# Another order of loads and steps, other kinds of pairs and wider copies in a retention-and-mixer kernel

## The chip, the core and the metric

One core of one Trainium2 chip runs the whole program. The metric is the device time of one execution in microseconds (us). The kernel before was timed in three runs; a fourth execution was profiled, and its own time is given beside its span (first to last instruction).

## What is computed

```python
# q, k, v: (4 batches, 8 heads, 768 tokens, 64); x: the attention output as (4, 768, 512)
gamma = 1.0 - 2.0 ** (-5.0 - np.arange(H))
for t in range(S):
    state = gamma * state + outer(k[:, :, t], v[:, :, t])      # 64 x 64 for each head
    y[:, :, t] = scale * q[:, :, t] @ state
...
wq = x @ w_q; wk = x @ w_k                                     # 512 -> 64
W_tok = scale * einsum('bsd,btd->bst', wq, wk)
mixed = einsum('bst,btd->bsd', W_tok, x)
out = np.maximum(mixed, 0.0) @ w_out                           # 512 -> 512
```

The first stage is a linear attention with a decay for each head. The second mixes all tokens of a batch without a softmax, so that it is computed through the 64 x 512 matrix wk^T x (called z) rather than through a 768 x 768 matrix.

## The kernel before

The 768 tokens of a batch are cut in three **pairs** of 256 tokens, so there are 12 pairs, 0 to 11, and three in a row make a batch. A pair has two chunks of 128 tokens, c = 0 and 1. q, k and v of a pair are 512 KB each and are loaded into one of 27 slots of a staging tile (`stage`). Products are taken in bf16 and gathered in the eight PSUM banks; bank 7 holds the running state.

All work is one list, `ORDER` (L16 to L60), that is walked once from front to back. Each token of it is a step: `name.pair.part:engine@banks=slot`. Every engine gets its steps in the order of the list and never overtakes, a step starts when what it reads is there and when what it overwrites has been read, and the semaphores for that are put in by the framework. The load queue (SP) issues its loads and the final stores in the order of the list as well. A load waits in the list for its slot to be read out and for room in the queue; where it stands among the steps of the engines does not matter. The engine letters are A (ACT), V (DVE) and P (POOL).

The steps of a pair, in the order in which its data flows:

- `Lk Lq Lv` load; `ck cv cq` cast to bf16 (`cv` also multiplies v with the inverse decay), part 0 and 1.
- `trk trq` transpose k and q on PE into one bank (eight 128x128 transposes), or, with an `a` behind the banks, into halves of two banks (sixteen 64-row ones). `ek eq` copy the results out (kT, qT).
- `sc` scores of half the heads, into two banks; `eat` multiplies them with the mask on DVE and leaves them in bf16.
- `st` adds k^T v of a chunk to the state in bank 7; `es` copies the state out.
- `ia` and `in` add the part of y within a pair and the part from the state, into two banks; `ex` scales y by the decay on DVE (x).
- `xt exT` transpose x and copy it out; `wqk ew` make wq and wk (m); `zm ez` make z of a batch; `mx` mixes; `r` applies the relu to a chunk; `pj` is the last product of a chunk (four matmuls of 512 columns); `eo` copies it to a staging slot; `S` stores.
- `fill.n@b` runs n matmuls on zeros; they keep PE busy and compute nothing. `W`, `WO` cast the weights that `LW`, `LO` load.

Each pair has a **kind** (L62), which says how its 256 tokens lie in the 128 partitions after loading. In the kinds R and 2 a partition holds two neighbouring tokens of each head, so that a DMA reads 512 B in one piece. For R the cast also moves half the rows, so that `ck` and `cv` take two instructions of 64 partitions for each part. For 2 a part is one instruction of 128 partitions, but `st` takes 16 matmuls in place of 8, `sc` and `ia` 16 in place of 8, and `in` 12 in place of 8. In M the k is loaded as in R, and v is loaded in four DMAs of 256 B pieces, which leaves `cv` one instruction a part. In N both k and v are read in 256 B pieces, and `ck` has one instruction a part as well.

Tiles come from pools of a fixed number of buffers (L69): `relu=4` buffers of one chunk each, `x=6`, `ks=6` and so on. A new tile waits until the oldest of its pool has been read for the last time.

Of the kernel before, what the change touches and what calls it, by code (L numbers as in the profile page):

```python
# [22 lines left out]
Lq.10=5 cv.3.1:P cq.5.0:P ia.0.1@56 fill.1@1 trk.2@1 fill.1@3 in.0.1@56 Lk.10=12 cq.2.1:A cq.2.0:A
sc.1.0@23 ek.2:V cv.4.0:P sc.1.1@01 trq.2@4 eq.2:A es.0.1:A ia.0.0@56 eat.1.0:V ex.0:V eat.1.1:V
cv.4.1:P fill.4@2 sc.2.1@34 cq.3.0:A cv.5.0:P sc.2.0@56 fill.2@2 st.1.0 es.1.0:A ck.3.0:A ck.3.1:A
Lv.10=6 Lq.11=8 ia.1.1@01 in.1.1@01 st.1.1 eat.2.1:V ck.6.0:P ia.1.0@01 in.1.0@01 trq.3@4 eat.2.0:V
xt.0@5 cv.5.1:P ex.1:V cq.7.1:P cq.7.0:P cv.6.1:P es.1.1:V exT.0:V eq.3:V trk.3@6 fill.2@2 in.2.0@01
cv.6.0:P Lv.11=9 st.2.0 ck.4.1:A ek.3:A xt.1@5 es.2.0:A exT.1:V ck.4.0:A ia.2.1@01 ia.2.0@01
in.2.1@01 ck.7.1:P ex.2:V st.3.0 fill.1@2 sc.3.0@56 trk.4@34a cq.4.1:A cv.7.1:P cv.7.0:P W:A trq.4@0
xt.2@1 ek.4:V sc.3.1@23 ck.8.1:P cq.8.0:P eat.3.0:V eq.4:V wqk.1@4 ew.1:V cq.5.1:A exT.2:A es.3.0:A  # L30
wqk.0@5 ck.8.0:P sc.4.0@01 trq.5@6 wqk.2@4 ck.5.1:A ew.0:A eat.4.0:V ew.2:V zm.0.0@5 sc.4.1@01
st.3.1 eat.3.1:V ck.5.0:A WO.0:A es.3.1:A trk.5@4 cq.9.1:P cv.8.0:P in.3.1@23 zm.0.1@5 ia.3.1@23
ia.3.0@23 eat.4.1:V ez.0:V cv.9.0:P cv.8.1:P st.4.0 ex.3:V ek.5:A es.4.0:A in.4.0@01 mx.0@45
in.4.1@01 ia.4.1@01 ia.4.0@01 eq.5:V WO.1:A st.4.1 xt.3@23a r.0.1:A pj.0.1@6 ex.4:V r.0.0:A es.4.1:A
ck.6.1:A eo.0.1:A=11 xt.4@01a cv.9.1:P mx.1@45 exT.3:V r.1.0:A cq.6.0:A sc.5.0@23 pj.0.0@6 st.5.0
exT.4:V r.1.1:V eat.5.0:V trk.6@4 ek.6:V sc.5.1@01 cq.6.1:A eo.0.0:A=11 trq.6@56a wqk.4@2 es.5.0:A
ia.5.0@34 eq.6:A in.5.0@34 in.5.1@34 eat.5.1:V trq.7@56a mx.2@01 ew.4:V eq.7:V r.2.1:A r.2.0:A
ck.7.0:A ia.5.1@34 wqk.3@2 ex.5:V pj.1.0@5 sc.6.1@01 st.6.0 eo.1.0:A=14 sc.6.0@34 xt.5@6 trk.7@5
ek.7:A eat.6.1:V pj.1.1@0 exT.5:V wqk.5@6 es.6.0:V st.6.1 eo.1.1:A=14 ew.5:A es.6.1:A ew.3:A
# [861 lines left out]
```

## Time and profile before

| | |
|---|---|
| three timed runs | 100.23, 100.91, 100.99 us; median 100.91 |
| the profiled execution, its own time | 100.14 us |
| its span | 98.4 us |
| granted TensorE clock, mean | 0.996 |
| busy: PE, DVE, ACT, POOL | 88.6, 74.4, 70.3, 51.8 us |
| HBM read, written | 20.19 MB, 6.29 MB |

A busy time is the union of an engine's instructions. PE's matmuls overlap in their pipeline and their ends are modelled, so the mean duration of one is longer than the step from one to the next; the step is read from rows of several in a row. PE's busy time contains the fills. DMA is the mean busy share of the 16 DMA engines of the core.

### The profile page before, as it was taken

Reading aid. Unit: us, or ns where it says so; the run is one execution under the profiler, and the core shown is the slowest. Engines: PE = TensorE matmul, PEld = TensorE weight load, DVE = VectorE, ACT = ScalarE, POOL = GpSimd, SP = SyncE. Lnnn points to the kernel's source line nnn. Section 1 sums busy time; section 2 is a strip of 40 time slices with the busy share of each in tenths; the row PEclk is TensorE's granted clock in tenths of the full one; section 3 lists DMA queues with packets and bytes.
Section 4 is the critical chain, followed back from the end, with each engine's and each line's share of the span. In section 5 each row is a group of like instructions: output and inputs, shape, how many; then the busy total and the mean of one; then the engine's idle time right before and its main releaser. Section 6 shows DMA issues by size and latency. Waiting matters only on the chain.

```text
span 98.4 us, 3827 instructions
## 1 busy us (share of the span) xinstructions
PE 88.6 (90%) x1626; PEld 59.9 (61%) x1642; DVE 74.4 (76%) x127; ACT 70.3 (71%) x124; POOL 51.8 (53%) x68
## 2 busy tenths in 40 slices
PE   5994899999869999999999988999999989999940
PEld 1333477487757776586887554786787766744410
...
DMA  1999999999998999999899799799905910690893
GB/s 26 282 385 368 367 363 361 343 327 282 293 330 256 303 317 348 354 336 293 255 337 309 177 323 323 159 244 273 361 21 205 402 46 0 245 391 14 323 397 132
DMA packets 37953, 26.73 MB, mean 272 GB/s; under 512 B 8240, under 2 KB 31792, under 8 KB 37936
## 3 DMA queue, kind: packets, MB, share of 16 engines
...
q10 hardware_dynamic: 528, 0.26, 0.9%
...
HBM read 20.19 MB, written 6.29 MB: 269 GB/s over the span
## 4 chain that ended last, share of the span: by engine, by line
PE 55%; SPq 20%; ACT 7%; DMA 6%; DVE 4%; issue 2%; POOL 1%; DVEq 0%; POOLq 0%
PE banks L826 19%; SPq L193 11%; DMA stage<-in_q_dram 6%; SPq L172 6%; PE banks L748 5%; PE banks L759 5%; PE banks L558 3%; PE banks L685 3%; SPq L200 3%; ACT relu L819 3%; PE banks L592 2%; PE banks L515 2%; PE banks L804 2%; DVE relu L821 2%; PE banks L631 2%
## 5 line engine op out<-in xcount | busy, mean ns | idle before, releaser
L401 POOL TENSOR_TENSOR vs<-stage,fv 64x512 bf16<-64x512 f32 x22 | 23.6, 1075 | 6.4 <-DMA stage<-in_v_dram 5.2
L576 DVE TENSOR_TENSOR at<-banks,maskR 128x1024 bf16<-128x1024 f32 x18 | 21.7, 1219 | 3.8 <-PE banks L558 3.8
L826 PE MATMUL banks<-wout_sb,relu 128*128 128x512 bf16 x84 | 22.9, 381 | 0.9 <-DVE relu L821 0.2
L147 ACT CAST ks<-stage 64x512 bf16<-64x512 f32 (+1 forms) x25 | 15.4, 618 | 4.7 <-DMA stage<-in_k_dram 4.3
L147 ACT COPY stage<-banks 128x512 f32<-128x512 f32 x19 | 11.0, 587 | 5.8 <-PE banks L826 5.7
L706 DVE TENSOR_TENSOR x<-banks,fy 128x1024 bf16<-128x1024 f32 x12 | 14.6, 1219 | 0.6 <-PE banks L685 0.3
L826 PEld LDWEIGHTS <-relu 128*128 128x128 bf16 x96 | 8.3, 99 | 9.3 <-issue 0.8
L148 POOL CAST ks<-stage 64x512 bf16<-64x512 f32 (+1 forms) x15 | 9.1, 609 | 6.4 <-DMA stage<-in_k_dram 5.8
L347 PE MATMUL banks<-warm 128*128 128x512 bf16 x34 | 10.9, 451 | 1.6 <-DVE warm L226 1.2
L819 ACT ACTIVATE relu<-banks 128x512 bf16<-128x512 f32 x18 | 10.0, 601 | 3.0 <-PE banks L804 1.5
L147 ACT CAST qs<-stage 128x512 bf16<-128x512 f32 x14 | 8.4, 618 | 1.5 <-DMA stage<-in_q_dram 1.3
L382 POOL TENSOR_TENSOR vs<-stage,fv 128x512 bf16<-128x512 f32 x6 | 6.2, 1047 | 5.4 <-DMA stage<-in_v_dram 5.4
L576 DVE TENSOR_TENSOR at<-banks,mask 128x1024 bf16<-128x1024 f32 x6 | 7.1, 1219 | 1.0 <-ACT ks L147 0.8
L147 ACT COPY kT<-banks 128x1024 bf16<-128x1024 bf16 x6 | 6.1, 1011 | 2.4 <-PE banks L473 1.7
L759 PE MATMUL banks<-wqk_w,xT 128*128 128x64 bf16 x96 | 7.5, 243 | 0.1
L558 PE MATMUL banks<-qT,kT 64*128 64x128 bf16 x144 | 6.8, 218 | 0.9 <-ACT kT L147 0.5
L347 PEld LDWEIGHTS <-warm 128*128 128x128 bf16 x38 | 3.8, 110 | 6.0 <-issue 3.0
L147 ACT CAST s<-banks 128x256 bf16<-128x256 f32 x16 | 6.0, 375 | 1.9 <-PE banks L592 1.9
L748 PE MATMUL banks<-xT,wqk_w 128*128 128x256 bf16 x48 | 7.3, 275 | 0.0
L148 DVE COPY qT<-banks 128x1024 bf16<-128x1024 bf16 x8 | 5.5, 686 | 2.0 <-PE banks L515 1.0
L148 POOL CAST qs<-stage 128x512 bf16<-128x512 f32 x9 | 5.4, 611 | 2.8 <-DMA stage<-in_q_dram 2.5
L592 PE MATMUL banks<-vs,ks 128*64 128x64 bf16 (+1 forms) x200 | 6.9, 198 | 0.0
...
## 6 DMA issues: line engine op xcount, KB each, us to landing
...
```

What stands on the lines that cost most here:

```text
L147: return nc.scalar.copy(out=out, in_=in_)
L148: return ENGINES[e].tensor_copy(out=out, in_=in_)
L193: eng.dma_start(out=to[g, hs], in_=fr[g, hs])
L347: nc.tensor.matmul(out=bank32(b), lhsT=warm[:, 0:128], rhs=warm, start=True, stop=True)
L401: eng.tensor_tensor(out=st["vs"][rows(j), c].rearrange("p hp x d -> p (hp x) d"), in0=src[rows(c), :, j], in1=fv[rows(c), cp, :, j].to_bro ...
L558: nc.tensor.matmul(out=at[:, x, hi, c], lhsT=kT[rows(x), hp, c], rhs=qT[rows(x), c, hp], start=(hi == 0 and c == 0), stop=(hi == 1 and c = ...
L576: ENGINES[e].tensor_tensor(out=st["at", half].rearrange("p x hi j t -> p x (hi j t)").rearrange("p x (n f) -> p x n f", n=n), in0=st["at_p ...
L706: ENGINES[e].tensor_tensor(out=dst, in0=src, in1=f.to_broadcast([128, 2, H, D]), op=ALU.mult)
L748: nc.tensor.matmul(out=ps[:, 128:384], lhsT=wqk_sb[:, a, 0 : 2 * DH], rhs=st["xT"][:, a].rearrange("p c t -> p (c t)"), start=(a == 0), st ...
L759: nc.tensor.matmul(out=wk[:, c], lhsT=st["xT"][:, a, c, :], rhs=wqk_sb[:, a, 2 * DH :], start=False, stop=(a == NDM - 1), skip_group_check ...
L819: nc.scalar.activation(out=st["relu", c], in_=src, func=ACT.Relu)
L826: nc.tensor.matmul(out=bank32(b[0]), lhsT=st["relu", c][:, a // 2, a % 2, :], rhs=wout_sb[:, a, :], start=(a == 0), stop=(a == NDM - 1),)
```

## The change

The list is another one: other engines for the casts and evictions, other banks, other places for the steps, and the loads in another order. The kinds of the pairs go from `R22RRR2RRMMM` to `RRR2RRMRRMMN`: the pairs 1 and 2 become R, pair 3 becomes 2, pair 6 becomes M, pair 11 becomes N. There are 32 fills in place of 38. `ck` and `cq` can now do both parts in one instruction (used by `ck.3`, `cq.4`, `cq.7`, `cq.11`), and so can `r` (used by `r.4` and `r.8`). The relu of a pair is one tile of twice the size with two buffers in place of four. `QF` is empty, so the branches on it in `trq` and `eq` are not taken.

The engines' work is now, in steps by letter: the 64-partition casts `ck` 24 on A, 14 on P and 2 on V (before 22, 12, 2), the 64-partition `cv` 26 on P and 2 on V (before 22 and 2), the other `cv` 10 on P (before 12), `eo` 16 on A and 8 on V (before 19 and 5), `r` 11 single and 2 double on A and 9 on V (before 18 and 6).

The order of the loads, before and after:

```
v0 k0 q0 q1 k1 k2 q2 v1 q3 k3 v2 k4 v3 W q4 q5 k5 v4 LO.0 LO.1 v5 k6 q6 q7 v6 k7 v7 k9 q8 k8 q9 v8 v9 k11 q10 k10 v10 q11 v11
v0 k0 q0 q1 k1 v1 q2 k2 q3 v2 k3 W k4 q4 v3 v4 LO.1 LO.0 k5 q5 v5 k6 q6 v6 k7 q7 v7 q9 k9 q8 k8 v8 k10 q10 v9 q11 k11 v10 v11
```

The diff, its lists cut to the stretches that the text speaks of:

```diff
-fill.15@6 cv.0.0:V Lk.0=1 ck.0.1:V Lq.0=2 ck.0.0:A Lq.1=3 Lk.1=4 Lk.2=5 Lq.2=6 Lv.1=7 fill.3@0
-trk.0@0 Lq.3=8 Lk.3=9 Lv.2=10 Lk.4=11 cq.0.1:V Lv.3=12 LW=13 Lq.4=14 Lq.5=15 Lk.5=16 cv.0.1:P
...
+fill.15@6 Lk.0=1 Lq.0=2 cv.0.0:P cq.0.0:V cv.0.1:V ck.0.0:A Lq.1=3 Lk.1=4 Lv.1=5 cq.0.1:P ck.0.1:A
+Lq.2=6 Lk.2=7 fill.1@0 st.0.0 fill.3@0 trk.0@01a cq.1.0:P fill.4@2 trq.0@23a ek.0:V es.0.0:V
+ck.1.0:V cv.1.0:P eq.0:A ck.1.1:A Lq.3=8 cq.1.1:A Lv.2=9 fill.4@4 sc.0.1@01 st.0.1 trk.1@2 eat.0.1:V
+trq.1@3 Lk.3=10 sc.0.0@01 eq.1:V eat.0.0:V LW=11 es.0.1:A ek.1:A sc.1.1@23 eat.1.1:V sc.1.0@45
+ck.2.1:P Lk.4=12 cq.2.1:A ck.2.0:A cq.2.0:A cq.3.0:A eat.1.0:V ia.0.1@01 cq.3.1:P cv.1.1:P fill.2@6
+trk.2@6 st.1.0 trq.2@2 Lq.4=13 in.0.1@01 eq.2:V ia.0.0@01 ex.0:V fill.2@3 trq.3@34a ek.2:A cv.2.0:P
+Lv.3=14 es.1.0:A Lv.4=15 eq.3:V sc.2.1@56 eat.2.1:V LO.1=16 ia.1.1@01 in.1.0@01 xt.0@2 sc.2.0@34
+cv.2.1:P st.1.1 LO.0=17 ck.3:A es.1.1:A in.1.1@01 ia.1.0@01 st.2.0 trk.3@5 es.2.0:A eat.2.0:V
+Lk.5=18 exT.0:A ck.4.0:A W:A ex.1:V in.2.1@34 in.2.0@34 ia.2.0@34 ia.2.1@34 Lq.5=19 ek.3:V ck.4.1:P
+fill.1@6 sc.3.0@56 sc.3.1@01 xt.1@2 ex.2:V wqk.0@3 xt.2@4 ew.0:A exT.2:A eat.3.1:V cq.4:P cv.3.0:P
+cv.3.1:P trq.4@0 trk.4@3 exT.1:V wqk.1@2 wqk.2@4 Lv.5=20 eq.4:A cv.4.0:P eat.3.0:V ek.4:V st.3.0
+ew.2:V ew.1:A sc.4.1@01 WO.0:A zm.0.0@2 cv.4.1:P sc.4.0@34 Lk.6=21 zm.0.1@2 es.3.0:V eat.4.1:V
+eat.4.0:V ez.0:A st.3.1 ia.3.0@01 ia.3.1@01 mx.0@56 es.3.1:A r.0.0:A WO.1:P in.3.1@01 cq.5.0:P
+mx.2@23 r.0.1:V ck.5.1:P st.4.0 r.2.0:A Lq.6=22 es.4.0:A r.2.1:V ia.4.1@45 ia.4.0@45 in.4.0@45
+mx.1@23 in.4.1@45 cq.5.1:A Lv.6=23 pj.0.1@6 ex.3:V trq.5@0 ex.4:V cv.5.0:P pj.0.0@1 eq.5:V ck.5.0:A
+trk.5@45a cv.5.1:P st.4.1 xt.3@0 Lk.7=24 eo.0.1:A=25 r.1.0:A r.1.1:V cq.6.0:P ek.5:V exT.3:V
...
+Lv.10=15 sc.10.1@34 cv.10.0:P eat.10.1:V in.9.1@12 ia.9.0@12 ia.9.1@12 trq.11@0 ex.9:V wqk.8@5
+trk.11@34a zm.2.0@6 st.9.1 Lv.11=16 eq.11:A ek.11:V cv.10.1:P ew.8:A zm.2.1@6 sc.10.0@01 sc.11.1@23
+xt.9@45a es.9.1:A ez.2:A st.10.0 pj.5.1@6 eat.10.0:V exT.9:A es.10.0:A eo.5.1:A=17 ia.10.1@01
+ia.10.0@01 eat.11.1:V mx.8@45 in.10.0@01 S.2 r.8:A in.10.1@01 cv.11.1:P cv.11.0:P sc.11.0@23 st.10.1
+wqk.9@6 ew.9:A S.1 eat.11.0:V es.10.1:A pj.8.0@4 S.4 S.0 S.5 S.3 ex.10:V ia.11.1@56 ia.11.0@56
...
+mx.9@56 mx.11@12 mx.10@34 S.6 S.8 r.11.1:V pj.7.0@0 r.11.0:A r.10.1:A eo.7.0:A=20 pj.11.1@1
+pj.11.0@2 S.7 r.10.0:V r.9.1:A eo.11.0:A=21 r.9.0:A eo.11.1:V=21 pj.10.1@0 eo.10.1:V=22 S.11.1
+S.11.0 pj.10.0@1 pj.9.1@6 S.10.1 eo.10.0:V=22 S.10.0 eo.9.1:A=23 S.9.1 pj.9.0@0 eo.9.0:A=23 S.9.0
...
-KINDS = "R22RRR2RRMMM"
+KINDS = "RRR2RRMRRMMN"
...
-    ks=6, vs=6, qs=4, kT=3, qT=3, at0=2, at1=2, s=4, x=6, xT=3, m=7, z=2, relu=4,
+    ks=6, vs=6, qs=4, kT=3, qT=3, at0=2, at1=2, s=4, x=6, xT=3, m=7, z=2, relu=2,
...
-    def ck(e, b, p, c):
+    def ck(e, b, p, c=None):
...
+            if c is None:
+                copy(
+                    e,
+                    st["ks"].rearrange("p hp j x d -> p hp x j d"),
+                    st["k_st"].rearrange("p (hp x j d) -> p hp x j d", hp=HP, x=2, j=2),
+                )
+                return
...
-    def cq(e, b, p, x):
+    def cq(e, b, p, x=None):
...
+            if x is None:
+                copy(
+                    e,
+                    st["qs"].rearrange("p u x d -> p x u d"),
+                    st["q_st"].rearrange("p (x u d) -> p x u d", x=2, u=U),
+                )
+                return
...
-    def r(e, b, p, c):
-        st = pairs[p]
-        st["relu", c] = new("relu", [128, 2, 2, C])
-        src = st["mx_ps"][:, :, :, c * C : c * C + C]
+    def r(e, b, p, c=None):
+        st = pairs[p]
+        if "relu" not in st:
+            st["relu"] = new("relu", [128, 2, 2, 2 * C])
+        ts = slice(0, 2 * C) if c is None else slice(c * C, c * C + C)
+        dst, src = st["relu"][:, :, :, ts], st["mx_ps"][:, :, :, ts]
...
-                lhsT=st["relu", c][:, a // 2, a % 2, :],
+                lhsT=st["relu"][:, a // 2, a % 2, c * C : c * C + C],
```

More of the change, by code (lines that the diff above doesn't have):

```diff
@@ L23 @@
[L23 to L39, printed above, removed]
@@ L66 @@
 PAD = 224
+QF = ()
 SPLIT = ()
@@ L506, in trq @@
         st = pairs[p]
+        if p in QF:
+            src = st["q_st"].rearrange("p (x u d) -> p u x d", x=2, u=U)
+            st["qtr"] = ps = two32(b).rearrange("p i (v n) -> p i v n", n=C)
+            for u in range(U):
+                nc.tensor.transpose(ps[:, u // 4, u % 4], src[:, u], ident_f)
+            return
         qs = st["qs"]
```

60 lines of the change are left out of this document (34 added, 26 removed).

## The prediction

> **What bounds the kernel now.** I read the page's shares, its slices of DMA and its groups first, then stretches of the span, then PE's idle time and order.
>
> ```profile
> PE 88.6 (90%) x1626; PEld 59.9 (61%) x1642; DVE 74.4 (76%) x127; ACT 70.3 (71%) x124; POOL 51.8 (53%) x68
> DMA  1999999999998999999899799799905910690893
> L347 PE MATMUL banks<-warm 128*128 128x512 bf16 x34 | 10.9, 451 | 1.6 <-DVE warm L226 1.2
> core 0: us, PE busy (x) PEld busy (x) DVE busy (x) ACT busy (x) POOL busy (x), PEclk, DMA share, GB/s
> 7.80:31.80 24.00, 21.28 (x465) 15.62 (x469) 19.61 (x24) 18.22 (x32) 11.57 (x14) 1.00 1.06 328
> 31.80:94.60 62.80, 61.26 (x1148) 42.10 (x1156) 48.86 (x58) 48.36 (x86) 36.21 (x43) 1.00 0.82 257
> 35.00:40.00 5.00, 4.84 (x119) 3.30 (x121) 5.00 (x8) 4.44 (x8) 4.39 (x6) 1.00 1.05 342
> 60.00:66.00 6.00, 6.00 (x131) 4.19 (x130) 5.48 (x7) 5.11 (x10) 4.27 (x7) 1.00 0.89 221
> 31.47 0.40 PE L558 MATMUL banks<-qT,kT 64*128 64x128 bf16 x8
> 88.08 6.52 PE L826 MATMUL banks<-wout_sb,relu 128*128 128x512 bf16 x27
> ```
>
> From 31.8 us to the end of the last `pj` at 94.6 PE stands still for 62.80 - 61.26 = 1.54 us, at full clock (1.00) and without fills. That stretch is bound by PE's own work. Before it PE is short of data: of its 10.9 us of fills and of its idle time nearly all lies ahead of 31.8. The DMA slices stay near full until late, but nobody on PE's path waits for them after 31.8. So the kernel ends sooner only if PE is further in its work at some early moment, has less work, or stands still less behind it. I compare the kernels at one landmark, the score half `sc.4.0` of pair 4 that ends at 31.47 + 0.40 = 31.87; I count 31.8, where the next step starts. What lies behind the last `pj` (eviction, store, 98.4 - 94.6 = 3.8 us) has the same form in both lists.
>
> **When data lands.** The loads are one stream, so the n-th load of the new list lands about when the n-th landed before (all but a few are 512 KB).
>
> ```profile
> 6.54 1.25 ACT L147 CAST ks<-stage 64x512 bf16<-64x512 f32 x2 [3.42 <-DMA stage<-in_k_dram]
> 14.99 2.05 POOL L382 TENSOR_TENSOR vs<-stage,fv 128x512 bf16<-128x512 f32 x2 [2.21 <-DMA stage<-in_v_dram]
> 20.34 2.05 POOL L382 TENSOR_TENSOR vs<-stage,fv 128x512 bf16<-128x512 f32 x2 [2.74 <-DMA stage<-in_v_dram]
> 23.21 2.16 POOL L401 TENSOR_TENSOR vs<-stage,fv 64x512 bf16<-64x512 f32 x2 [0.82 <-DMA stage<-in_v_dram]
> 27.32 0.61 POOL L148 CAST qs<-stage 128x512 bf16<-128x512 f32 x1 [1.95 <-DMA stage<-in_q_dram]
> 70.64 3.04 POOL L392 TENSOR_TENSOR vs<-stage,fvm 128x512 bf16<-128x512 f32 x3
> 77.84 0.63 PE L685 MATMUL banks<-vs,at 128*128 128x64 bf16 x16
> ```
>
> The steps of the first five rows waited for their load: 2nd load 6.5, 8th 15.0 (1.41 a load), 11th 20.3, 13th 23.2, and the 14th behind the weights 27.3. In the new order q0 (3rd) is there at 7.9, v1 (6th) at 12.2, k2 (8th) at 15.0, v2 (10th) by 18.5, k3 (11th) at 20.3, k4 behind the weights near 23, q4 near 24.4, v3 at 27.3, v4 near 28.6. v1 comes 2.8 us sooner, v2 1.8 sooner, v3 4.1 later.
>
> **The early stage, followed in the new list.** Steps from one start to the next:
>
> ```profile
> 18.43 3.48 DVE L576 TENSOR_TENSOR at<-banks,mask 128x1024 bf16<-128x1024 f32 x3
> L148 DVE COPY qT<-banks 128x1024 bf16<-128x1024 bf16 x8 | 5.5, 686 | 2.0 <-PE banks L515 1.0 <-PE banks L519 1.0
> L401 DVE TENSOR_TENSOR vs<-stage,fv 64x512 bf16<-64x512 f32 x2 | 2.1, 1065 | 0.9 <-DMA stage<-in_v_dram 0.9
> L148 DVE CAST ks<-stage 64x512 bf16<-64x512 f32 x2 | 1.6, 800 | 0.0
> L147 ACT COPY xT<-banks 128x1024 bf16<-128x1024 bf16 x5 | 5.1, 1011 | 1.9 <-PE banks L721 1.9
> 27.75 0.61 ACT L147 CAST wqk_w<-stage 128x512 bf16<-128x512 f32 x1
> 28.27 0.41 ACT L340 ACTIVATE wqk_w<-stage 128x256 bf16<-128x256 f32 x1
> 28.61 0.45 PE banks L715 x8
> 32.42 0.44 PE banks L748 x4
> 32.85 0.46 PE banks L759 x8
> 50.47 0.37 PE banks L592 x16
> 29.06 0.33 PE banks L558 x8
> ```
>
> DVE first: from q0 at 7.9 its steps up to `ek.4` are eight `eat` and three `ex` at 3.48 / 3 = 1.16, six 1024-column copies at 0.60 (686 ns less the 0.08 that neighbours overlap), `cv.0.1` 2.1, `ck.1.0` 1.6, and 1.4 for `cq.0.0`, `ek.0` and `es.0.0`: 12.8 + 3.6 + 2.1 + 1.6 + 1.4 = 21.5, ending at 29.4. At each step I compared with the producer (`sc.1.0` is through near 15.6, `sc.2.0` near 21.5) and found DVE late rather than waiting. ACT: k3 at 20.3, `ck.3` 1.05 as one instruction (unseen there; by the equal cast of `WO`, quoted below, and not below one half of 0.62 or above two), the state copies until 22.8, `exT.0` 0.9, `ck.4.0` 1.25, `W` 0.9: done at 26.0. PE can then start `wqk.0`, and its list runs on without a gap: three `wqk` at 0.44 + 0.46, `xt.2`, `trq.4`, `trk.4` at 0.5, `st.3.0` 0.37 and `sc.4.1` 0.33 make 4.9, so 30.9. At that moment the new kernel has done what the old one has at 31.8, and `wqk.2` on top, which the old one does later. Lead: 0.9 + 0.9 = **1.8 us**.
>
> **PE's work behind the landmark.**
>
> ```profile
> 36.28 0.25 PE banks L592 x8
> 36.53 0.22 PE banks L631 x8
> 51.86 0.12 PE banks L641 x4
> 51.98 0.24 PE banks L652 x8
> 62.01 0.34 PE banks L721 x16
> L147 ACT CAST wout_sb<-stage 128x1024 bf16<-128x1024 f32 x2 | 2.1, 1047 | 0.0
> ```
>
> A kind-2 pair costs 0.37 against 0.25 for each `st` and 0.12 + 0.24 against 0.22 for each `in`. Left over are pair 6 before (0.12 x 2 + 0.14 = 0.38) and pair 3 after (0.26): -0.12. `sc` and `ia` take twice the matmuls at about half the step each and I count them even. Of the transposes two fewer have the split form (0.34 against 0.45): +0.22. The twelve others are moves. Sum +0.1, so work gives nothing either way.
>
> **Where PE will stand.** Two steps that read one `mx` result follow one another:
>
> ```profile
> ACT relu L819 <- DVE relu L821: 1.4, 2, 0.9
> DVE relu L821 <- ACT relu L819: 1.1, 2, 1.0
> L821 DVE TENSOR_SCALAR relu<-banks 128x512 bf16<-128x512 f32 x6 | 4.1, 686 | 1.4 <-ACT relu L819 1.1 <-PE banks L804 0.3
> L819 ACT ACTIVATE relu<-banks 128x512 bf16<-128x512 f32 x18 | 10.0, 601 | 3.0 <-PE banks L804 1.5 <-DVE relu L821 1.4
> ```
>
> All four pairs whose `r` was split over ACT and DVE show it; the new list splits nine (0, 1, 2, 3, 5, 6, 7, 10, 11), so a result is out 0.6 + 0.69 after `mx`. I followed each: `ia.4.1` waits 0.35 for `r.0.1`, `mx.4` 0.35 for `r.3.1`, `wqk.7` 0.1. With two buffers `r.1.0` also waits for both `pj.0`: ACT holds it until `pj.0.0` ends, DVE holds `r.1.1` behind it, then comes `ek.5`, and `sc.5.0` starts 0.7 late. The other splits have a `pj` or a `wqk` in front that covers them. Together 1.5; bounds 0 and 9 x 0.6 = 5.4. `r.4` and `r.8` as one instruction are unseen: between 0.6 and 1.2 on ACT, taken as 1.05, with PE busy on `in.7.0` or `wqk.9` meanwhile. The whole `cq` on POOL is unseen too (0.61 to 1.22, I take the upper end); POOL runs ahead of PE there. I add 0.5 for stops that I have not found, so 2.0 against 1.54: -0.46.
>
> POOL's four more `cv` of 64 partitions (2.16 for two) and two more `ck` (1.25 for two) are 5.6 us beside PE. POOL was busy for 51.8 of 98.4 us and stood idle ahead of loads; that idle time covers them, and without it they would come one to one where PE wants `vs`. k11 and v6 are now read in 256-byte pieces. In 60 to 66 us, where such loads run, 512 KB at 221 GB/s take 2.37 us against 1.53 at 342: at most 0.84 more each, at least nothing. I take 0.84, since that row also holds 0.89 of DMA share. v11 was there by 71.6 (the last two `vs` of that row), is then there by 73.3, and two `cv` at 1.01 make 75.3. Before, PE came to `ia.11.1` at 77.84, 16.8 ahead of its end; the new list has a `wqk` less and an `st` more behind it, so 93.3 - 16.1 = 77.2. That is 1.9 in hand. v10 lands one such load sooner, 70.9, its `cv` end at 72.9, and PE wants it 3.7 us of steps ahead of `ia.11.1`, at 73.5, with `st.10.0` a microsecond before that on half of it. Little to spare there, and that is a rival.
>
> The Trainium skill (DMA: Bandwidth & Descriptors, section Why small descriptors are slow) gives 11 cycles in place of 8 for a 256-byte piece, 27% of it overhead. By that, as an estimate, the two loads would cost about 0.4 us each and the last load would be there near 72.4.
>
> **Sum.** 1.8 - 0.1 - 0.46 = 1.24, I say 1.3 us sooner in the profiled execution: 100.14 - 1.3 = 98.84. The four times before (100.14, 100.23, 100.91, 100.99) have their middle at 100.57, 0.43 above the profiled one; so I predict a median of **99.3**, 1.6% under 100.91. The three timed runs lie 0.8% apart, so about 1% is what can be told from no change: under 99.9 is faster, over 101.9 slower.
>
> **Rivals.**
> 1. *The last loads are late.* If the two loads and the reads around them cost 1.7 us each, not 0.84, v10 and v11 come 1.7 later, and PE stands 1.5 at `ia.10.1`. Lead gone: 100.8, same. For it: no slack at v10. Against: POOL did not wait ahead of the last three `vs` at 70.64.
> 2. *The early lead is half.* DVE has 21.5 us in a row without a gap, while it stood idle for 4.4 of 24 us before (24.00 - 19.61). Each stop goes through to `ek.4`. Half the lead: 100.2, same.
> 3. *Relus take turns and PE waits them out* (other side). Place: the nine split pairs, `r.1` with its two buffers above all. If PE reaches the next user of the banks too early at all nine, it stands 5.4 us where 1.5 is in my sum: 99.3 + 3.9 = 103.2; at six of nine 101.4. Over 101.9 from seven on. For it: all splits before show the turn, with waits of up to 0.9 and 1.0 us. Against: before, PE lost 0.2 us to a relu (the row of the PE group `L826`).
> 4. *PE stands still less than before.* With 0.5 in place of 2.0 the gain is 2.8: 97.8.
>
> ```profile
> L826 PE MATMUL banks<-wout_sb,relu 128*128 128x512 bf16 x84 | 22.9, 381 | 0.9 <-DVE relu L821 0.2
> ```
>
> **Chances.** Forecast 0.44, of which 0.08 ends within 1%; rival 1 0.18, rival 2 0.13, rival 3 with its neighbours (several of these stops at once) 0.15, rival 4 0.10. Faster 0.36 + 0.10 = 0.46. Slower 0.15 and a quarter of rival 1, 0.04: 0.19, with 0.01 of rival 2: 0.20. Same 0.34. The range goes from just under rival 4 to rival 3 at some seven splits: 97.6 to 102.2.
>
> **What would show it.** Right: `sc.4.1` ends near 31 with all three `wqk` behind it; DVE with hardly any idle time from 8 to 29; PE's idle time from there to its end near 2 us, with a gap ahead of `sc.5.0`; PE ends near 93.3. Wrong: PE waits for `vs` from 70 on (rival 1), DVE waits for PE before 29 (rival 2), waits of PE on relu in the sum over 3 us (rival 3).

## The result and the profile after

The changed kernel took 100.75 us (median of 20 runs, 100.27 to 101.53) against 100.39 for the kernel before (20 runs, 99.14 to 104.8): a ratio of 1.0074, 95% interval 1.0045 to 1.0104. I had predicted 99.3. Ratios leave out executions that took over 1.5% more than the fastest of their kernel, so they need not be those of the medians. The profiled execution of after is the longest of its 20 (101.53 us, span 99.7), so the distance of 1.39 us between the two profiles is nearly twice the 0.74 us of the ratio. Its PE line, its DMA slices and the stretch from the landmark to the last `pj`:

```profile
PE 86.4 (87%) x1516; PEld 59.1 (59%) x1532; DVE 75.6 (76%) x132; ACT 67.5 (68%) x116; POOL 56.9 (57%) x73
DMA  0999999999999999999999999989995740055993
30.90:96.00 65.10, 60.76 (x1091) 41.88 (x1102) 50.67 (x61) 46.79 (x81) 36.14 (x42) 1.00 0.84 260
```

The early part of the timeline, two rows of DVE, one of ACT and the landmark on PE (start, duration):

```profile
8.11 0.43 DVE L148 CAST qs<-stage 128x512 bf16<-128x512 f32 x1 [3.40 <-DMA stage<-in_q_dram]
28.64 0.68 DVE L148 COPY kT<-banks 128x1024 bf16<-128x1024 bf16 x1
25.74 0.41 ACT L343 ACTIVATE wqk_w<-stage 128x256 bf16<-128x256 f32 x1
30.45 0.40 PE L592 MATMUL banks<-qT,kT 64*128 64x128 bf16 x8
```

DVE's chain runs from 8.11 to 29.32, `W` is done at 26.15 and the landmark `sc.4.1` ends at 30.85, 1.02 us before its counterpart of before (31.87), with all three `wqk` done. The early lead is there. What follows is where it goes. Every stop of PE of more than 0.15 us behind the landmark, first in before, then in after:

```profile
59.31 0.62 PE L558 MATMUL banks<-qT,kT 64*128 64x128 bf16 x16 [0.51 <-ACT kT L147]
80.45 1.04 PE L826 MATMUL banks<-wout_sb,relu 128*128 128x512 bf16 x3 [0.20 <-DVE relu L821]
```

```profile
33.87 0.39 PE L838 MATMUL banks<-m,z 64*128 64x256 bf16 x4 [0.86 <-ACT z L147]
35.67 0.60 PE L719 MATMUL banks<-vs,at 128*128 128x64 bf16 x15 [0.35 <-DVE relu L857]
37.03 0.81 PE L862 MATMUL banks<-wout_sb,relu 128*128 128x512 bf16 x3 [0.16 <-issue]
41.17 0.62 PE L592 MATMUL banks<-qT,kT 64*128 64x128 bf16 x16 [0.89 <-DVE kT L148]
...
56.70 0.39 PE L838 MATMUL banks<-m,z 64*128 64x256 bf16 x4 [0.43 <-ACT relu L855]
...
63.85 0.60 PE L782 MATMUL banks<-xT,wqk_w 128*128 128x256 bf16 x4 [0.23 <-DVE relu L857]
...
90.45 5.50 PE L862 MATMUL banks<-wout_sb,relu 128*128 128x512 bf16 x23 [0.30 <-ACT relu L855]
```

The row with "issue" (there are four of them) is a `pj` of which one matmul record is missing, three in place of four; I do not count it. The six others sum to 3.06 us, the two of before to 0.71. Last `pj`: 94.60 before, 95.95 after. So 95.95 - 30.85 = 65.10 and 94.60 - 31.87 = 62.73: the new list lost 2.37 behind its landmark, 2.35 of it in listed stops, and ended 1.35 later. Without the listed stops both take the same, 62.0, although after had one `wqk` less to do.

The first of these stops, 0.86 us at `mx.0`, eats PE's lead. The same step in three other executions whose list is that of after up to there (runs e2, l3 and p3 below):

```profile
33.75 0.39 PE L837 MATMUL banks<-m,z 64*128 64x256 bf16 x4 [0.35 <-ACT z L146]
```

```profile
33.97 0.39 PE L838 MATMUL banks<-m,z 64*128 64x256 bf16 x4 [0.44 <-ACT z L147]
```

```profile
33.86 0.39 PE L838 MATMUL banks<-m,z 64*128 64x256 bf16 x4 [0.95 <-ACT z L147]
```

Their landmarks end at 31.24, 31.37 and 30.75, that of after at 30.85, but `mx.0` starts between 33.75 and 33.97 in all four: a PE that comes half a microsecond sooner stands about half a microsecond longer. What holds `mx.0` is a load, as the first experiment shows; the cast of what it brings starts between 32.38 and 32.60 in these executions.

The scaling `ex` of a pair on DVE is a good marker, because there is one for each pair. Here `ex.2`, `ex.4`, `ex.5` and `ex.11` of before, then `ex.2`, `ex.3` with `ex.4`, `ex.5` and `ex.11` of after:

```profile
25.93 1.23 DVE L706 TENSOR_TENSOR x<-banks,fy 128x1024 bf16<-128x1024 f32 x1 [0.24 <-PE banks L652]
...
38.14 1.21 DVE L706 TENSOR_TENSOR x<-banks,fy 128x1024 bf16<-128x1024 f32 x1
45.25 1.22 DVE L706 TENSOR_TENSOR x<-banks,fy 128x1024 bf16<-128x1024 f32 x1
...
80.31 1.21 DVE L706 TENSOR_TENSOR x<-banks,fy 128x1024 bf16<-128x1024 f32 x1
```

```profile
24.64 1.23 DVE L740 TENSOR_TENSOR x<-banks,fy 128x1024 bf16<-128x1024 f32 x1
36.22 2.35 DVE L740 TENSOR_TENSOR x<-banks,fy 128x1024 bf16<-128x1024 f32 x2
46.23 1.22 DVE L740 TENSOR_TENSOR x<-banks,fy 128x1024 bf16<-128x1024 f32 x1
...
81.57 1.22 DVE L740 TENSOR_TENSOR x<-banks,fy 128x1024 bf16<-128x1024 f32 x1
```

After is 1.29 us ahead at `ex.2`, 0.7 at `ex.4`, 0.98 behind at `ex.5` and 1.26 behind at `ex.11`. The loss falls between 25 and 46 us, where 2.10 of the 3.06 us of stops lie as well. (The two lists do not have quite the same steps of PE ahead of each `ex`, so these distances are good to a few tenths.)

### The profile page after: what moved, and what is told of

Same layout as the page of the kernel before. It is cut to its first block, busy times and chain, and to the rows that moved or that the text cites. A ratio compares the mean times of both kernels' runs of the same rounds, so it can differ in the third digit from the quotient of the medians.

```text
span 99.7 us, 3617 instructions
## 1 busy us (share of the span) xinstructions
PE 86.4 (87%) x1516; PEld 59.1 (59%) x1532; DVE 75.6 (76%) x132; ACT 67.5 (68%) x116; POOL 56.9 (57%) x73
## 3 DMA queue, kind: packets, MB, share of 16 engines
q1 hardware_dynamic: 39488, 26.22, 85.1%
## 4 chain that ended last, share of the span: by engine, by line
PE 52%; DVE 19%; ACT 15%; issue 6%; DMA 5%; SPq 0%; DVEq 0%; ACTq 0%
PE banks L862 16%; DVE at L610 7%; ACT ks L147 6%; PE banks L782 6%; PE banks L793 5%; DMA stage<-in_k_dram 5%; DVE relu L857 4%; PE banks L592 4%; DVE x L740 3%; PE banks L719 3%; PE banks L541 3%; ACT relu L855 3%; PE banks L819 2%; PE banks L626 2%; PE banks L749 2%
## 5 line engine op out<-in xcount | busy, mean ns | idle before, releaser
L147 ACT CAST ks<-stage 64x512 bf16<-64x512 f32 (+2 forms) x26 | 16.5, 633 | 4.8 <-DMA stage<-in_k_dram 4.5
L855 ACT ACTIVATE relu<-banks 128x512 bf16<-128x512 f32 (+1 forms) x13 | 8.6, 667 | 4.3 <-DVE relu L857 2.8
L148 POOL CAST qs<-stage 128x512 bf16<-128x512 f32 (+1 forms) x11 | 8.1, 743 | 5.8 <-DMA stage<-in_q_dram 3.7
L857 DVE TENSOR_SCALAR relu<-banks 128x512 bf16<-128x512 f32 x9 | 6.2, 689 | 5.3 <-ACT relu L855 4.0
L719 PE MATMUL banks<-vs,at 128*128 128x64 bf16 x176 | 7.6, 193 | 1.5 <-DVE at L610 0.5
L719 PEld LDWEIGHTS <-at 128*128 128x128 bf16 x176 | 6.4, 98 | 3.4 <-issue 1.8
L147 ACT COPY xT<-banks 128x1024 bf16<-128x1024 bf16 x8 | 8.0, 1013 | 0.4 <-ACT z L147 0.4
L592 PEld LDWEIGHTS <-kT 64*128 64x128 bf16 x176 | 5.2, 94 | 4.0 <-issue 1.5
L147 ACT CAST m<-banks 128x384 bf16<-128x384 f32 x10 | 4.7, 480 | 4.1 <-PE banks L793 3.2
L626 PEld LDWEIGHTS <-ks 128*64 128x64 bf16 (+1 forms) x176 | 4.5, 110 | 3.9 <-ACT ks L147 1.9
```

Source lines behind the costliest of these rows:

```text
L147: return nc.scalar.copy(out=out, in_=in_)
L148: return ENGINES[e].tensor_copy(out=out, in_=in_)
L592: nc.tensor.matmul(out=at[:, x, hi, c], lhsT=kT[rows(x), hp, c], rhs=qT[rows(x), c, hp], start=(hi == 0 and c == 0), stop=(hi == 1 and c = ...
L626: nc.tensor.matmul(out=state_ps[rows(x), hp, :], lhsT=st["ks"][rows(c), hp, j, x, :] if two else st["ks"][:, c, hp, x, :], rhs=st["vs"][ro ...
L719: nc.tensor.matmul(out=y[:, x, c, hp, :], lhsT=at[:, x, hi, c, :], rhs=vr[:, c, hp, x, :], start=first(p, x), stop=False, skip_group_check ...
L855: nc.scalar.activation(out=dst, in_=src, func=ACT.Relu)
```

## Experiments: the stops of PE

Theory A: the standstill was mis-sized, and each stop has a cause in the list that can be taken away. Theory B, against the prediction: PE's own work is not the bound behind the landmark, so stops and leads on PE do not come back one to one.

**WO.0 later.** `mx.0` waited for `ez.0` (z), which stood on ACT behind the cast of `WO.0`, and that waited for its load (ACT, after):

```profile
32.49 1.04 ACT L147 CAST wout_sb<-stage 128x1024 bf16<-128x1024 f32 x1 [2.72 <-DMA stage<-in_moe_w_out_dram]
33.45 0.37 ACT L147 CAST z<-banks 128x256 bf16<-128x256 f32 x1
```

```diff
-... sc.4.1@01 WO.0:A zm.0.0@2 ... r.0.0:A WO.1:P
+... sc.4.1@01 zm.0.0@2 ... r.0.0:A WO.0:A WO.1:P
```

> The new kernel with one step moved: WO.0 (the cast of the second half of w_out, which waits for its load until 32.4 us) stands behind r.0.0 on ACT, so that ez.0 no longer queues behind it. Theory A (late data held by ACT's order: q5 lands at 36.8 and ACT passes the lateness through cq.5.1, ck.5.0, eo.0.1, r.1.0 to r.1.1 and ek.5 on DVE): PE's stop of 0.86 ahead of mx.0 goes away, but sc.5.0 still starts near 41.2, since what holds it starts from q5; the time moves by less than 0.3 us. Rival (every stop of PE goes straight to the end): 0.8 us faster.

Measured: 101.14 us, ratio 1.0107 (1.0069 to 1.0145). The stop at `mx.0` is gone. Two others stand in the trace:

```profile
35.94 0.39 PE L837 MATMUL banks<-m,z 64*128 64x256 bf16 x4 [0.61 <-DVE relu L856]
...
40.74 0.62 PE L591 MATMUL banks<-qT,kT 64*128 64x128 bf16 x16 [0.88 <-DVE kT L147]
```

The first is new, at `mx.1`, since `r.2.0` now stands on ACT behind the moved cast; the second, at `sc.5.0`, is as long as in after. So nothing came back: the ratio is no lower than after's 1.0074, the rival falls, and the first part of the theory (the stop at `mx.0` goes, the time does not) holds.

**Four buffers for the relu.**

```diff
-    ... m=7, z=2, relu=2,
+    ... m=7, z=2, relu=4,
```

> The new kernel with four relu buffers of the double size in place of two, nothing else. Theory A: r.1.0 still stands behind cq.5.1, ck.5.0 and eo.0.1 on ACT and starts near 39.2, sc.5.0 near 41.2, time within 0.3 us of the new kernel. Rival B (the two buffers cost it): sc.5.0 0.7 to 0.9 sooner and the time 0.7 us faster.

Measured: 100.23 us, ratio 0.998 (0.9939 to 1.0021), about 0.9% under after. The stop at `sc.5.0` is gone (it starts at 40.30), so its cause is the one that the prediction named: with two buffers `r.1.0` waits for `pj.0.0`, and `ek.5` is queued behind `r.1.1`. The late q5, which theory A blamed here and in e1, is not the cause; rival B holds. Of its own landmark (31.24) and its last `pj` (94.85) 63.61 us lie apart; less 1.60 of listed stops that is 62.0 again. Here the removed stops did come back.

**Both, and r.1.0 earlier.** The two edits above, and:

```diff
-... in.4.1@45 cq.5.1:A ... eo.0.1:A=25 r.1.0:A r.1.1:V
+... in.4.1@45 r.1.0:A cq.5.1:A ... eo.0.1:A=25 r.1.1:V
```

> The new kernel with both of the above and r.1.0 ahead of cq.5.1 on ACT, so that it waits neither for q5 nor for pj.0. Theory A: PE's stops ahead of mx.0 (0.86) and sc.5.0 (0.89) are both gone, sc.5.0 starts near 40.2, and the time falls by 0.8 to 1.5 us. Rival B: no more than the second kernel of this call. Rival C (the stops only move on to later steps): within 0.4 us of the new kernel.

Measured: 100.42 us, ratio 1.0058 (1.002 to 1.0095), no better than the buffers alone. Landmark 30.64, last `pj` 94.69.

**Two more stops covered.**

```diff
-... in.4.0@45 mx.1@23 in.4.1@45 r.1.0:A cq.5.1:A Lv.6=23 pj.0.1@6 ex.3:V
+... in.4.0@45 in.4.1@45 cq.5.1:A Lv.6=23 pj.0.1@6 mx.1@23 r.1.0:A ex.3:V
-... in.7.0@01 mx.4@23 in.7.1@01 st.7.1 Lq.11=12 pj.3.1@6
+... in.7.0@01 in.7.1@01 st.7.1 mx.4@23 Lq.11=12 pj.3.1@6
```

> after with four buffers for the relu tile, `WO.0` behind `r.0.0`, and two steps of PE moved behind others that cover the relu that they wait for: `mx.1` behind `pj.0.1` (0.61 us in e3_wo_relu4_r1) and `mx.4` behind `st.7.1` (0.37). Theory (standstill was the wrong term of the sum): PE's stops behind `sc.4.1` fall from the 1.8 us of e3_wo_relu4_r1 to about 0.9, and the time from 100.4 to 99.6, under before by 0.5 to 0.8%. Rival (the relus' turn moves on: `r.1` is later, so `sc.5.0` or `pj.1` waits): stops stay at 1.5 or more, 100.2 or more.

Measured: 100.26 us, ratio 1.0014 (0.9979 to 1.0049), 0.4% under e3 with intervals that overlap. In the profiled executions the stops of PE fell from 2.05 to 1.25 us, and PE ended at 94.65 in place of 94.69. The rows of `mx.4` and `wqk.7` in e3, then those of `mx.5` and `wqk.7` in this kernel:

```profile
55.61 0.40 PE L837 MATMUL banks<-m,z 64*128 64x256 bf16 x4 [0.37 <-ACT relu L854]
...
62.76 0.60 PE L781 MATMUL banks<-xT,wqk_w 128*128 128x256 bf16 x4 [0.22 <-DVE relu L856]
```

```profile
60.57 0.39 PE L837 MATMUL banks<-m,z 64*128 64x256 bf16 x4 [0.15 <-ACT xT L146]
62.71 0.60 PE L781 MATMUL banks<-xT,wqk_w 128*128 128x256 bf16 x4 [0.22 <-DVE relu L856]
```

The 0.37 at `mx.4` is gone; `wqk.7` starts 0.05 us sooner and still waits 0.22. PE gave the time back in pieces. What the two early stops had won was gone at `trk.5`, whose first matmul starts at 38.47, 0.48 us sooner than in e3, and whose second waits for a cast of k5 on ACT:

```profile
38.90 0.41 PE L498 MATMUL banks<-identity,ks 64*128 64x64 bf16 x15 [0.23 <-ACT ks L146]
```

It stands 0.43 us behind the first, of which the view shows 0.23 as idle, because the modelled end of a matmul hides the rest. What `mx.4` had won went between there and `wqk.7`, 0.15 of it at `mx.5`. First evidence for B, from one pair of executions.

**The buffers alone, in the old order.** After's functions, with before's list and kinds:

```diff
+    ... m=7, z=2, relu=2,      # one tile of both chunks for a pair
-    ... m=7, z=2, relu=4,      # one tile for each chunk
```

> The list and the kinds of before, with the relu tile of after: one tile of both chunks for a pair, two buffers in place of four of half the size. Theory (the two buffers hurt only with the new order, in which `r.2` comes ahead of `r.1` and so `r.1` needs the buffer of pair 0): here `r.1` takes the second buffer and `r.2` comes long after both `pj.0`, so no wait of ACT on `pj` ahead of `sc.5.0`, and 100.3 within 0.3 us. Rival (the double tile costs in any order): PE stands 0.5 us or more longer at relu or score steps, 100.8 or slower.

Measured: 101.14 us, ratio 1.0024 (0.9984 to 1.0064). No wait at `sc.5.0`; one late stop of 0.75 us for a relu at 91.67. Not told apart from no change.

## Experiments: keeping the lead

**The new start with the old rest.** After's list up to `sc.4.1`, then what is left of before's list in its order, the loads in a mix of both orders (up to v3 as after, then q5 v4 k5 LO.0 LO.1 v5 and on as before), four double relu buffers. Against after:

```diff
-KINDS = "RRR2RRMRRMMN"
+KINDS = "RRR2RR2RRMMM"
-... ew.1:A sc.4.1@01 WO.0:A zm.0.0@2 cv.4.1:P sc.4.0@34 ...
+... ew.1:A sc.4.1@01 cq.5.0:P cv.4.1:P ... trq.5@6 ck.5.1:A eat.4.1:V zm.0.0@5 sc.4.0@01 ...
```

> The new list up to sc.4.1, the landmark of the prediction, and from there the steps of the old list in the old order, engines and banks (halves of pair 4 swapped); loads in the new order up to v3, then q5 v4 k5 LO.0 LO.1 and the old order; pair 3 of kind 2, pair 6 of kind 2, the last three M; four relu buffers. If the lead of 1.8 us at the landmark is real and the loss lies in the new list behind it: PE's end near 93 us, 1.0 to 1.8 us faster than the kernel before. If the lead is paid for by data that comes later (k5, v4, weights): no faster than the kernel before, with PE waiting between 32 and 40 us.

Measured: 102.87 us, ratio 1.0272 (1.02 to 1.0344), here over all six executions. In the profiled execution (100.54 us, the fastest of six, at clock 1.00) PE stood 2.10 us at `trq.5` for `cq.5.0`, queued on POOL behind `cv.4.0`; it took 0.3 us more than the median of before, 100.28. The five others took 102.4 to 104.4 with granted clocks of 0.958 to 0.983 (last section), so the 1.0272 is not the price of the order alone.

**q5 first (e5), then k5 too (e6).** In e6 `trk.5` also moves behind `ia.3.1`, and `WO.0` behind `es.4.0`.

```diff
-... eq.4:A cv.4.0:P eat.3.0:V ... sc.4.1@01 cq.5.0:P cv.4.1:P ... st.3.1 ck.5.0:A WO.0:A es.3.1:A trk.5@4
+... eq.4:A cq.5.0:P cv.4.0:P ck.5.0:P eat.3.0:V ... sc.4.1@01 cv.4.1:P ... st.3.1 es.3.1:A
```

> The mixed list of e4_hybrid, with the cast of the first half of q5 on POOL moved ahead of `cv.4.0`. Theory (stop goes on to the next late operand): PE no longer stands 2.1 us at `trq.5`, but `trk.5` then waits for the casts of k5, which ran from 31.48 to 33.98 in e4_hybrid, so `trk.5` starts near 34.0 and not at 34.57; the span gains about 0.6, to 98.2 (100.0 with what lies around it) in an execution at full granted clock. Rival 1 (the 2.1 us come back whole): span 96.7, 98.5. Rival 2 (clock): five of the six executions of e4_hybrid show a granted clock of 0.958 to 0.983 and took 102.4 to 104.4; if the dense list itself is what lowers the clock, these executions show it as well and the median stays above 101.5.

> e5_q5_first with more help for pair 5: `ck.5.0` goes from ACT to POOL behind `cv.4.0`, `trk.5` moves behind `ia.3.1`, and `WO.0` moves behind `ek.5` and `es.4.0` on ACT. Theory (the early lead can be kept if every operand of the following 5 us is early): `trk.5` starts near 33.3 with at most 0.3 us of waiting, `mx.0` waits up to 0.5 for `ek.5`, and the end comes 1.3 to 1.8 us before that of e4_hybrid: span 97.0 to 97.5, 98.8 to 99.3 at full granted clock. Rival 1 (another operand is late by as much): span 98.3 or more. Rival 2 (clock): granted clock under 0.99 and a median of 101 or more whatever PE's idle time is.

Measured: 101.56 us, ratio 1.002 (0.9973 to 1.0068), and 100.74 us, ratio 1.0027 (0.9987 to 1.0066). In the first the stop went on to `trk.5`, as expected; in the second to `pj.0.1`, whose relu was queued on ACT behind both halves of `WO` (the one row of e5, then the one of e6):

```profile
34.23 0.62 PE L492 MATMUL banks<-identity,ks 128*128 128x128 bf16 x8 [0.96 <-ACT ks L146]
```

```profile
38.40 1.89 PE L861 MATMUL banks<-wout_sb,relu 128*128 128x512 bf16 x4 [1.07 <-ACT relu L854]
```

**These covered as well.**

```diff
-... sc.4.1@01 cv.4.1:P cv.5.0:P ... eq.5:V WO.1:A st.4.1 ... ek.8:A sc.8.0@56 sc.8.1@34 pj.3.1@0 pj.4.0@1
+... sc.4.1@01 cv.4.1:P WO.1:P cv.5.0:P ... eq.5:V st.4.1 ... ek.8:A pj.3.1@0 sc.8.0@56 sc.8.1@34 pj.4.0@1
```

> e6_q5_k5 with two of its stops covered: `WO.1` goes from ACT to POOL behind `cv.4.1` (PE stood 1.07 us at `pj.0.1` for a relu that was queued on ACT behind both halves of `WO`), and `pj.3.1` moves ahead of `sc.8.0`, where PE stood 0.51 us for `ek.8`. Theory (each stop removed on PE comes back one to one): 1.4 to 1.6 us less standstill than e6_q5_k5, so at full clock a span of 97.0 to 97.4 where e6_q5_k5 had 98.5 to 98.8, 98.9 to 99.2 us, and a ratio to before of 0.985 to 0.992. Rival (clock or late loads take it back): PE's idle time falls by over 1 us but the time by less than 0.5, 100.3 or more.

Measured: 100.96 us, ratio 1.0068 (1.003 to 1.0107): the theory fell. `ex.4`, `ex.5` and `ex.11` of this kernel, and the stop that replaced the one at `sc.8.0`:

```profile
36.93 1.22 DVE L739 TENSOR_TENSOR x<-banks,fy 128x1024 bf16<-128x1024 f32 x1
44.97 1.21 DVE L739 TENSOR_TENSOR x<-banks,fy 128x1024 bf16<-128x1024 f32 x1
...
81.11 1.21 DVE L739 TENSOR_TENSOR x<-banks,fy 128x1024 bf16<-128x1024 f32 x1
```

```profile
59.31 1.02 PE L861 MATMUL banks<-wout_sb,relu 128*128 128x512 bf16 x4 [0.45 <-DVE x L739]
```

It is 1.21 us ahead of before at `ex.4`, 0.28 at `ex.5` and 0.80 behind at `ex.11`, with a remaining list that is before's own but for a few moves. Of the 0.93 us lost between `ex.4` and `ex.5` 0.28 is a listed stop; of the 1.08 lost from there to `ex.11` 0.83 are, 0.54 of them at `trq.8` for a cast on POOL. The moved `pj.3.1` needs the bank that `ex.7` has to read first, so the old stop of 0.51 became one of 0.45.

**The second move alone, in before.**

```diff
-... r.4.1:A ek.8:A sc.8.0@56 sc.8.1@34 pj.3.1@0 pj.4.0@1
+... r.4.1:A ek.8:A pj.3.1@0 sc.8.0@56 sc.8.1@34 pj.4.0@1
```

> before with one step moved: `pj.3.1` ahead of `sc.8.0`, where PE stood 0.51 us for the copy of kT on ACT. Theory (one to one): the stop goes, PE ends 0.5 us sooner, 99.5 to 99.9 and a ratio of 0.995. Rival (another stop follows, or the loads decide): ratio 1.000 within 0.3%.

Measured: 100.94 us, ratio 1.0095 (1.0061 to 1.0129). One step moved, slower by as much as the whole change. A stop of 0.45 for `ex.7` stands here too. The profiled execution is the longest of its 13 (103.03 us) and has a further stop of 1.83 us behind a late load (shown with the loads below); why the others are slower than before by more than the stops differ is not settled.

**The kinds alone, in the old list.** In before:

```diff
-KINDS = "R22RRR2RRMMM"
+KINDS = "RRR2RRMRRMMN"
```

> The list of before, unchanged, with the kinds of after (`RRR2RRMRRMMN`). Theory (the kinds are innocent, the order makes the loss): within 0.4 us of before, 100.3. Rival 1 (the 64-partition casts and the loads in 256-byte pieces make the loss): 100.8 or slower, with PE waiting for `vs`, `ks` or the copies of pairs 1 and 2. Rival 2 (the kinds bring the early lead by themselves): under 99.8.

Measured: 104.45 us, ratio 1.0358 (1.0288 to 1.0429), the largest loss of all. Its waits of PE:

```profile
PE banks L591 <- POOL vs L381: 2.4, 2, 2.0
```

This is the state step `st.3.0`, at 28.06. With pairs 1 and 2 as R their four `cv` parts take two 64-partition instructions each (2.16 for two by before's rows, in place of 1.02), some 4.5 us more on POOL ahead of `cv.3`. The mean granted clock of that profile was 0.975, and right behind this stop it was 0.50 for 3.4 us (last section), which costs PE up to 1.7 us of work, as an estimate. So the kinds are not innocent, since POOL's casts hold PE for 2.4 us in this order, but how much of the 3.6% is theirs and how much the clock's is not separated.

## Experiments: is PE's own work the bound?

**PE's work taken away.** One or two of the four matmuls of each `pj` of the pairs 0 to 5 left out:

```diff
+        n = NDM - 1 if p < 6 else NDM      # NDM - 2 in p2
-        for a in range(NDM):
+        for a in range(n):
```

> before, with one of the four matmuls left out of each `pj` of the pairs 0 to 5 (their output misses a quarter of the last product's sum; nothing else is changed, the evictions and stores keep their size). This takes 12 x 0.23 = 2.8 us of work off PE between 38 and 75 us. Theory 1, the one of the prediction (behind its landmark the kernel is bound by PE's own work): the end comes 2.8 us sooner, about 97.5 and a ratio of 0.972. Theory 2 (loads and evictions keep nearly the same pace as PE, so that PE's time comes back as new stops): under 1.2 us, 99.2 or more, with PE's stops between 35 and 75 us grown by over 1.5 us.

> As p1_before_pj3, with two of the four matmuls left out of these `pj`: 5.5 us of work off PE. Theory 1: 94.8, a ratio of 0.945. Theory 2: no more than 1.0 us sooner than p1_before_pj3, so 98.2 or more.

> after, with the same matmuls left out as in p1_before_pj3 (2.8 us of PE's work). Theory 1: 98.0, a ratio to before of 0.98. Theory 2 (other engines and the loads set the pace of the new list more than of the old one): less comes back than in p1_before_pj3, under 1.0 us, so 99.8 or more.

| | PE work taken off | ratio to before | comes to |
|---|---|---|---|
| p1, in before | 2.8 us | 0.9924 (0.9883 to 0.9965) | 0.8 us, 27% |
| p2, in before | 5.5 us | 0.9849 (0.9784 to 0.9915) | 1.5 us, 27% |
| p3, in after | 2.8 us | 0.9961 (0.992 to 1.0003), after itself 1.0074 | 1.1 us, 40% |

Over all executions the medians are 100.34, 99.35 and 99.98 us, with 100.15 for before, so the gains are rather smaller than larger. Theory 1, the prediction's, falls. Theory 2 holds for p1 and p2; it missed p3, which gained no less than p1, so the new list is no further from PE's work than the old one. In p2, PE over the stretch of before, `ex.4`, `ex.5` and `ex.11`, and the four largest stops behind 32 us:

```profile
31.80:94.60 62.80, 58.01 (x1134) 40.12 (x1132) 48.70 (x58) 48.59 (x87) 35.95 (x43) 1.00 0.83 260
```

```profile
38.08 1.21 DVE L706 TENSOR_TENSOR x<-banks,fy 128x1024 bf16<-128x1024 f32 x1
45.18 1.22 DVE L706 TENSOR_TENSOR x<-banks,fy 128x1024 bf16<-128x1024 f32 x1
...
79.31 1.22 DVE L706 TENSOR_TENSOR x<-banks,fy 128x1024 bf16<-128x1024 f32 x1
```

```profile
39.35 0.41 PE L721 MATMUL banks<-identity,x 64*128 64x64 bf16 x16 [0.36 <-DVE x L706]
...
53.68 0.41 PE L519 MATMUL banks<-ident_q,qs 64*128 64x64 bf16 x16 [0.39 <-POOL qs L148]
54.59 0.39 PE L804 MATMUL banks<-m,z 64*128 64x256 bf16 x4 [0.50 <-ACT z L147]
58.52 0.62 PE L558 MATMUL banks<-qT,kT 64*128 64x128 bf16 x16 [0.94 <-ACT kT L147]
```

PE is busy for 58.01 of the 62.80 us where it was busy for 61.26. Between `ex.4` and `ex.5` lie the two `pj` of pair 0 with 0.92 us less work, and the distance is 7.10 us where it was 7.11. DVE's x and relu, ACT's z and kT and a cast on POOL each name a stop; the one at `sc.8.0` grew from 0.51 to 0.94. I read this as: they were nearly as late as PE all along.

**Bytes taken off the late loads.** Half of each load of the pairs 8 to 11 left out, in before, with p2's edit, and in after:

```diff
-            load(name[1], args[0], int(slot))
+            load(name[1], args[0], int(slot), 0 if args[0] >= 8 else None)
```

> before, with half of the bytes left out of each load of the pairs 8 to 11 (the other half of the slot keeps what an earlier load left there; steps, casts and PE's work are unchanged). These are the last twelve loads, some 3 MB, and what is loaded from about 45 us on comes sooner, the last by several us. Theory 1 (PE's own work is the bound, loads are hidden): no change, 100.2 and a ratio of 1.00 within 0.3%. Theory 2 (PE and the loads run at nearly the same pace): a gain, but a small one, since PE's work is then the bound: 0.3 to 1.0 us. Theory 3 (the loads alone set the pace): over 2 us.

> p2_before_pj2 (5.5 us of work taken off PE) and l1_before_half together. Theory 2 (PE and the loads at nearly the same pace): more than the two gains added, at least 1.2 us under p2_before_pj2, ratio 0.972 or less. Theory 4 (evictions and casts on ACT, DVE and POOL are what keeps PE's time): no more than the sum of both, 0.98 or more, with PE's stops named by ACT and DVE as in p2_before_pj2.

> after, with the same bytes left out of the loads of the pairs 8 to 11 (two of its loads, of k11 and v11, are among those read in 256-byte pieces). Theory 1: no change from the ratio of 1.007. Theory 2: a gain of 0.3 to 1.0 us, a ratio of 0.998 to 1.004. If the late loads were what the new order lost by (rival 1 of the prediction), over 1.2 us and a ratio under 0.995.

Measured: 100.46 us and a ratio of 0.9997 (0.9959 to 1.0034); 99.16 and 0.9857 (0.9798 to 0.9916), where p2 alone had 0.9849; 100.94 and 1.0054 (1.0015 to 1.0093), where after had 1.0074. In the ratios the loads from about 45 us on hold nothing, in either list and with PE lightened. Single executions show that one of them is not far behind. In the profiled one of p1 (102.43 us) PE stood 2.12 us at `wqk.7`, whose bank `eq.9` had to read first, and `eq.9` is queued on ACT behind `cq.10.1`, which waited for the load of q10 (PE, then ACT):

```profile
65.08 0.60 PE L748 MATMUL banks<-xT,wqk_w 128*128 128x256 bf16 x4 [2.12 <-ACT qT L147]
```

```profile
63.50 0.62 ACT L147 CAST qs<-stage 128x512 bf16<-128x512 f32 x1 [2.70 <-DMA stage<-in_q_dram]
```

The same stop is 1.83 us in e11, 0.26 in p2 and 0.92 in q1 below; in before, l1 and l2 there is none. In l2 the other stops have the same names as in p2, with 0.76 us for z on ACT and 0.94 for kT.

**ACT lightened too.** p2 with the relus of the pairs 0 to 5 on the half of the columns that `pj` still reads:

```diff
+        n = 1 if p < 6 else 2
-        src = st["mx_ps"][:, :, :, c * C : c * C + C]
+        src = st["mx_ps"][:, :, :n, c * C : c * C + C]
```

> p2_before_pj2 with the relus of the pairs 0 to 5 cut to the half of the columns that their `pj` still reads (12 instructions of 256 columns in place of 512; 10 on ACT, 2 on DVE). From 0.60 us each I estimate about 0.35, so 3 us of work off ACT and 0.6 off DVE between 38 and 62 us. Theory 4 (the work and the queues of ACT and DVE keep PE's time): at least 0.7 us under p2_before_pj2, a ratio of 0.978 or less, with the stops of PE on ACT between 50 and 60 us (kT, z) shorter by 0.5 us or more. Rival (POOL, the early loads or PE's own hidden waits keep it): no change, 0.985 within 0.4%.

Measured: a median of 99.4 us (97.51 to 102.05, six runs) where before had 100.21, with no interval; p2 had a median of 99.35 where before had 100.15, so no gain over p2 shows. In the profiled execution (98.35 us) the stop for z grew to 0.75, that for kT fell to 0.68 only, and that behind the load of q10 was 0.92. Inconclusive: whether it is the work of ACT and DVE or only the order of their queues that holds PE stays open, as does the part of the loads before 45 us.

## Why the prediction was wrong

The landmark came where it was said, at 30.85 for 30.9. The stretch behind it was to take 93.3 - 30.9 = 62.4 us and took 65.10 in the profiled execution. In the terms of the sum, 1.7 of these 2.7 us are the standstill (PE idle for 4.34 - 0.64 = 3.70 us, for 2.0) and 1.0 is PE's work, which did not fall as said (point 3). The work was counted one to one on the premise of point 1, which is the step that failed first; the standstill missed the load behind `mx.0` besides.

1. **The bound, the step that failed first.** "That stretch is bound by PE's own work" was read from 61.26 busy of 62.80 us. In p1 and p2 about a quarter of the work taken off PE came back as time: 0.8 of 2.8 us (0.4 to 1.2 by the interval) and 1.5 of 5.5 (0.9 to 2.2). With it went what was read from the kernel before and carried over, that nobody on PE's path waits for loads after 31.8: in the new list `mx.0` waits for the load of `WO.0` through ACT, so that up to 0.95 us of PE's lead is lost there. The Trainium skill (Perfetto Trace Analysis, section Identifying the Most-Contended Engine) says that a matmul's busy share is no good measure of how near PE is to its limit, and points to the share of the weight loads, beside the share of peak arithmetic. By that row PE was at 42.10 of 62.80, 67%, with DVE at 48.86, 78%. The runs agree with the warning; I quoted both numbers and used only the first.
2. **The early lead of 1.8 us: right at the landmark.** DVE's chain ended at 29.32 (29.4 said), `W` at 26.15 (26.0), the landmark at 30.85 (30.9). The rival of half a lead did not come. But e9 shows a lead of 1.21 us at `ex.4` gone by `ex.11`: carrying it to the end unchanged was an error of the same kind as point 1.
3. **PE's work, +0.1 behind the landmark, with `wqk.2` done earlier.** Together that should have been 0.8 less outside stops; it was 62.04 against 62.02. (By busy time: 60.4 in the sum, 60.76 and the 0.64 of the missing records measured.) The records of single steps are too incomplete (83 of 96 for `pj`) to say which steps took it. e10 suggests small waits that no row shows.
4. **The standstill, 2.0 us: too small.** Listed stops 3.06; all idle time of the stretch 65.10 - 60.76 = 4.34, of which 0.64 are the four missing records. The 3.70 left is what compares with the 2.0, since before's 1.54 in the same sum was all idle time. Those that I had followed came nearly as said: `ia.4.1` 0.35 (0.35), `sc.5.0` 0.89 (0.7), `mx.4` 0.43 (0.35), `wqk.7` 0.23 (0.1), together 1.90 for 1.5. Not foreseen were `mx.0`, 0.86, and 0.30 at the end, for which I had put 0.5. e2 confirms the cause at `sc.5.0`, e1 that at `mx.0`. Part of the 3.70 belongs to this execution: e2 and l3 stood 0.35 and 0.44 at `mx.0`.
5. **Loads by count.** The first rows held to 0.2 us (q0 at 8.1 for 7.9), q4 came 1.8 late (its cast starts at 26.22, for 24.4), and v11 0.9 sooner than said:

```profile
26.22 1.04 POOL L148 CAST qs<-stage 128x1024 bf16<-128x1024 f32 x1 [0.92 <-DMA stage<-in_q_dram]
...
72.44 2.04 POOL L405 TENSOR_TENSOR vs<-stage,fvn 128x512 bf16<-128x512 f32 x2 [1.96 <-DMA stage<-in_v_dram]
```

   The estimate by the Trainium skill (DMA: Bandwidth & Descriptors, section Why small descriptors are slow) was 72.4 for v11, and its cast starts at 72.44, but this agreement is in part luck. The Trainium skill adds 3 cycles to every piece, so a 512-byte piece pays them too; with 22 against 19 cycles the two loads cost, as an estimate, 0.24 us each and v11 is due near 72.1. Besides, the 71.6 that both start from was only an upper bound, since nothing waited for v11 before. Rival 1 (late loads) did not decide: l3 gains 0.2%, within its interval.
6. **Rival 3 (relus in turn) was the nearest**, on the right side but too dear: PE waited 0.35 + 0.43 + 0.23 + 0.30 = 1.31 us for relus by name, and 0.89 more through the two buffers, not 5.4. That the time fell into the range is no merit of the mechanism: the sign of the forecast was wrong.
